# An identity matmul adds the residual, and ScalarE copies the sum out, in the late steps of two attention layers

## The chip, the cores and the metric

The kernel runs on one core of one Trainium2 chip. Five engines work side by side, each through its own instructions in order: TensorE (PE in the profile; its weight loads stand apart as PEld), VectorE (DVE), ScalarE (ACT), GpSimd (POOL) and SyncE (SP), which here only issues transfers (DMA). They meet through semaphores. The metric is device time in microseconds (us): the kernel before takes 1805.18 us, the median of three runs (1801.99 to 1808.54).

## The reference

Four layers on x of 2048 rows by 640 columns: attention, spectral mixing, attention, spectral mixing, each on the layer-normed input and added to it.

```python
def _A_ref(x, wqkv, wo):            # 32 heads of 20; 8 keys per row, 2 rows apart
    q, k, v = (x @ wqkv)...
    logits = einsum("bhsd,bhswd->bhsw", q, kg) * scale
...
    o = einsum("bhsw,bhswd->bhsd", softmax(logits), vg)
    return o @ wo
def _B_ref(x, ...):                 # real part of a 2-D DFT
    a, b = x @ dft_hid_re.T, x @ dft_hid_im.T
    return dft_seq_re @ a - dft_seq_im @ b
x = x + _A_ref(_layernorm(x), A_wqkv, A_wo)
x = x + _B_ref(_layernorm(x), ...)
x = x + _A_ref(_layernorm(x), A_wqkv, A_wo)
x = x + _B_ref(_layernorm(x), ...)
```

## The kernel before

**Data.** The 2048 rows are 4 chunks (c = 0 to 3) of 4 tiles (j = 0 to 3) of 128 rows; a tile is 128 partitions by 640 columns. Products that must be nearly exact are made of reduced-precision operands (fp32r): each operand is split into a high part and a remainder, and three matmuls (PASSES: high x high, high x low, low x high) accumulate in one PSUM bank. A bank holds 512 fp32 columns; they are named by tags (m0, m1, t0, t1, xt, aux0, aux1, pq).

**An attention layer** (`layer_a`, run as layer 0, from about 10 to 400 us, and as layer 2, from about 890 to 1290 us) is a plan of numbered steps. `at(step, phase, fn, ...)` (line 257) puts a piece of work in a step and a phase; a loop then goes through the steps -7 to 66 and, within a step, through the phases in the fixed order below (line 807), and issues every engine's instructions in that order. An engine's queue is therefore the plan read step by step, phase by phase:

```python
"peT0 dma evac hi pe peL pe2 fin red0 dma2 qk sA sB av0 sD red1 sE sC exp evacA actL evacO actl sF av1 qc"
" dmaw dmas misc dmac dmar pe3w pe3"
```

In each step, for a half head group: DVE multiplies q and k windows (L424, reading q from a PSUM copy that ACT makes, `q_copy` L397, phase qc of the step before), POOL halves that product (L426), DVE reduces it to logits (L432); DVE's softmax parts (L447 to L457) stand around ACT's exp (L440, phase exp), DVE multiplies the weights with v (L462), and POOL sums that in three passes (L477 to L479) into the output `oo`. The windows of k and v (`w_load`, L410, five buffers, phase dmaw) and q (`q_load`, L389, which waits for the q copy before it to free the buffer) come by DMA through SP's queue, in order.

**The output product.** A finished chunk of `oo` is transposed on PE (L320, from PSUM back by ACT: L324 the high part, then PE subtracts it by a negative identity, L328, and ACT copies the remainder, L343) into `oT`. `wo_mm` (L502) multiplies a tile of `oT` with the output weights: 15 matmuls of 320 columns for each half, the halves in the two banks aux0 and aux1, then `wo_add` sums the bank and the residual in DVE (`Stats.add`, L152: one instruction for a half, with an accumulator for the row sum) into the residual's tile `xr`, and stores it (L516). The residual comes by `r_load` (L188) or, for chunk 2, with `stage_load` (L488 and L489, into `r1_3`, so that it shows as tile `r`). Then `wo_stats` on ACT (L157 mean, L159 squares, L163), `wo_fin` on POOL (L167 the root), and the normalisation for the next layer: `ln_hi` on ACT (L175, L184 apply, L864 the high part), `ln_lo` on POOL or DVE (L868).

Chunks 0 and 1 go through this early. The **late steps** are those of chunk 2 (tiles 0 to 3 in steps 52 to 55) and of the first two tiles of chunk 3 (steps 60 and 61). Tiles 2 and 3 of chunk 3 follow behind the last step. From step 49 on, PE also runs the next layer's spectral products (`z_mm`, L918, five matmuls of 512 columns at a time, phase pe3, behind everything else of its step); their constants are split by ACT and DVE (L890, L903) in layer 0 and come ready by DMA in layer 2 (L895), into buffers that PE's earlier products must have left. Their order over the steps is written out by hand in `ZTHIRDS`.

In the late steps, a tile with its product in step w has: the product in phase pe3w of w, the sum on DVE in phase misc of w + 1, statistics on ACT in w + 2, the root in w + 3, the normalisation in w + 4 (chunk 2) or w + 3 (chunk 3).

Of the kernel before, what the change touches and what calls it, by code (L numbers as in the profile page):

```python
# [13 lines left out]
AF = mybir.ActivationFunctionType  # L14
# [58 lines left out]
def tile_layers(ctx: ExitStack, tc: tile.TileContext, x, wqkv, wo, cs, wre, wim, out):  # L73
    nc = tc.nc
# [4 lines left out]
    ps = ctx.enter_context(tc.tile_pool(name="ps", bufs=1, space=PSUM))  # L79
# [8 lines left out]
    def T(shape, tag, dt=F32, bufs=1, pool=None):  # L88
        return (pool or sb).tile(shape, dt, tag=tag, name=nm(tag), bufs=bufs)
# [7 lines left out]
    ident = T([P, P], "ident")  # L97
# [32 lines left out]
    class Stats:  # L130
# [18 lines left out]
        def add(self, j, e, xt, ps):  # L149
            o = xt[:, e * 320 : (e + 1) * 320]  # L150
            acc = (self.rstd, self.nmr)[e][:, j : j + 1]
            nc.vector.scalar_tensor_tensor(o, ps, 1.0, o, op0=ALU.mult, op1=ALU.add, accum_out=acc)  # L152

        def added(self, j, xt):
            nmean = self.nmean[:, j : j + 1]
            two = self.sums[:, :, j]
            nc.scalar.activation(two, two, AF.Copy, scale=-1.0 / D, accum_out=nmean)  # L157
            junk = T([P, D], "junk", mybir.dt.bfloat16)
            nc.scalar.activation(junk, xt, AF.Square, bias=nmean, accum_out=self.var[:, j : j + 1])  # L159
            self.var_eps(j)  # L160
# [74 lines left out]
    def layer_a(li, stats, handoff, prev):  # L235
        xin, xout = xs[li], xs[li + 1]
        first = li == 0
        ly = li // 2
        nstats = [None] * NC
# [12 lines left out]
        oT = {}  # L252
        xr = {}
# [3 lines left out]
        def at(step, phase, fn, *args):  # L257
            plan.setdefault((step, phase), []).append((fn, args))
# [32 lines left out]
        def tp(step, kind, c, j, k0, k1, bank, col=0, tag=None):  # L291
            if step not in pieces:
                pieces[step] = []
                at(step, "peT0", pc_pe, step)
                at(step, "hi", pc_hi, step)
                at(step, "peL", pc_sub, step)
                at(step, "actL", pc_lo, step)
            pieces[step].append((kind, c, j, k0, k1, bank, col, tag))
# [194 lines left out]
        def wo_mm(c, j, banks, e0=0, e1=2, k0=0, k1=KD):  # L493
            if e0 == 0 and k0 == 0:
                oT[(c, j, "m")] = []
            for e in range(e0, e1):
# [3 lines left out]
                for i, (a, b) in enumerate(PASSES):  # L500
                    for k in range(k0, k1):
# [5 lines left out]
                            stop=(i, k) == (2, KD - 1),  # L507
                        )

        def wo_add(c, j, e0=0, e1=2):  # L510
            for e in range(e0, e1):
                if e == 0 and j == 0:
                    nstats[c] = Stats()
                nstats[c].add(j, e, xr[(c, j)], oT[(c, j, "m")][e][:, :320])
            if e1 == 2:
                nc.sync.dma_start(xout[c][:, j, :], xr[(c, j)])  # L516
# [172 lines left out]
        while len(gs) < NGRP:  # L689
            if st % 2 == 0 and len(tx) < NC * NJ:  # L690
                c, j = divmod(len(tx), NJ)
# [46 lines left out]
        for c in range(2):  # L738
            for j in range(NJ):
                a = OUTP[ly][c][j]  # L740
                tp(a, "o", c, j, 0, 2, "t1", 0, "s0" if (c, j) == (1, 3) else "ot")
                tp(a, "o", c, j, 2, 5, "t0")
                at(a + 1, "dmar", r_load, c, j, "xa" if (c, j) == (1, 3) else "xr")
                for e in range(2):
                    at(a + 2 + e, "pe2", wo_mm, c, j, ("aux0", "aux1"), e, e + 1)
                    at(a + 3 + e, "misc", wo_add, c, j, e, e + 1)
                at(a + 5, "actl", wo_stats, c, j)
            at(a + 6, "fin", wo_fin, c, 0, 4)
            for j in range(NJ):
                t = LNS[ly][c] + (2 - c) * j  # L750
                if c == 0:
                    at(t, "dma2", handoff.ln_load, c, j)
                else:
                    at(t + STG[0], STG[1], stage_load, c, j)
                at(t, "actl", handoff.ln_hi, c, j, nstats)
                at(t + 1, "misc", handoff.ln_lo, c, j)
        for c, w, xtags in (
            (2, (52, 53, 54, 55), None),
            (3, (60, 61), ("xa", "xa")),
        ):  # L760
            for j in range(NJ):
                if c == 2:
                    tp(48, "o", c, j, 0, 3, ("xt", "t0", "t1", "m0")[j], 0, ("ot", "s1", "r1_2", "r1_2")[j])
                    tp(52, "o", c, j, 3, 5, f"aux{j // 2}", 256 * (j % 2))
                else:
                    tp(58 if j < 2 else TA, "o", c, j, 0, 3, f"aux{j % 2}", 0, ("ot", "s1", "zo0", "zo1")[j])
                    tp(60 if j < 2 else 67, "o", c, j, 3, 5, "aux0" if j < 2 else "pq", 256 * (j % 2))
                if j < len(w):
                    if xtags:
                        at(w[j], "dmar", r_load, c, j, xtags[j])  # L770
                    at(w[j], "pe3w", wo_mm, c, j, ("aux1", "aux0") if c == 3 else ("aux0", "aux1"))
                    at(w[j] + 1, "misc", wo_add, c, j)
                    at(w[j] + 2, "actl", wo_stats, c, j)
                    at(w[j] + 3, "fin", wo_fin, c, j, j + 1)
                    at(w[j] + 3 + (c == 2), "actl", handoff.ln_hi_own, c, j, xr, nstats)
                    at(w[j] + 4 + (c == 2), "misc", handoff.ln_lo, c, j)
# [34 lines left out]
        with tc.manual_schedule(engines=ENGINES):  # L811
            if first:
                prologue_first()
            nc.vector.tensor_copy(mk, mask)
            for s in range(LEAD0[0], last + 1):
                for ph in PHASES:
                    for fn, args in plan.pop((s, ph), ()):
                        fn(*args)
            pc_pe(67)
            pc_hi(67)  # L820
            pc_lo(67, True)
            wo_mm(c, 2, None, 0, 2, 3)
            wo_mm(c, 3, ("pq", "aux0"))
            wo_add(c, 2)
            wo_stats(c, 2)
            wo_fin(c, 2, 3)
            if first:
                handoff.c_hl(14)
            handoff.z_mm(13, None)
            handoff.ln_tail(c, 2, xr, nstats)  # L830
            wo_add(c, 3)
            handoff.ln_lo(c, 2)
            handoff.z_mm(14, None)
            wo_stats(c, 3)
            wo_fin(c, 3, 4)
            if first:
                handoff.c_hl(15)
            handoff.ln_tail(c, 3, xr, nstats)
            handoff.ln_lo(c, 3)
            handoff.z_mm(15, None)  # L840
# [414 lines left out]
    st0 = [None] * NC  # L1255
    b1, b2 = LayerB(1), LayerB(3)
    layer_a(0, st0, b1, None)
    st2 = [None] * NC
    b1.run(st2)
    layer_a(2, st2, b2, b1)  # L1260
    b2.run(None)
    b2.ytile(NT - 1, 0, None)
# [56 lines left out]
```

## Time and profile before

| | us |
|---|---|
| median of three runs | 1805.18 |
| lowest, highest | 1801.99, 1808.54 |
| the profiled execution, its own time | 1805.45 |
| its span, first to last instruction | 1803.7 |
| ACT in the span | 819.3 busy (45%) |
| DMA of the 16 engines, mean | 235 GB/s |

The granted TensorE clock of that execution was 0.992 of full speed on average.

How to read what follows. A row of the page's groups has the line of the kernel, the engine, the operation, output <- input by the kernel's tile names (their numbers left out), the shape and the count, then the busy time of the group and the mean duration of one in ns; matmuls overlap, so busy time divided by count is the distance from one to the next. A row of the timeline has the start in us from the span's start, the duration in us, the engine and the same names; in brackets the idle time just before it and what ended that. A row of the chain of waits has the start, the length and the work that the end was waiting for. A row of the list of waits has the total in us, how many times, and the longest. Fp32 and fp32r operands of PE both show as f32.

### The profile page before, as it was taken

What the parts mean: (1) busy time and instruction counts of PE and PEld (TensorE: products, weight loads), DVE (VectorE), ACT (ScalarE), POOL (GpSimd) and SP (SyncE); (2) the same over time, 40 slices, a digit from 0 to 9 for tenths busy, and PEclk for the clock granted to TensorE, in tenths of its full rate; (3) what the DMA queues carried; (4) which work ended last, traced back from release to release, by engine and by line L of the source; (5) the groups of instructions that cost most, each with busy time, mean ns of one, the idle gap of its engine ahead of it and who ended that gap; (6) DMA issues with size and microseconds to landing.
All of it is one profiled execution on the core that took longest, in us unless ns stands there. A gap on an engine that the chain in (4) does not pass through costs nothing.

```text
span 1803.7 us, 26494 instructions
## 1 busy us (share of the span) xinstructions
PE 1747.6 (97%) x8798; PEld 1508.5 (84%) x8798; DVE 1391.6 (77%) x2135; ACT 819.3 (45%) x1708; POOL 633.2 (35%) x591
## 2 busy tenths in 40 slices
PE   9999997989999999999999999999899999999999
PEld 7879886877888888888888889878787888888888
DVE  5899899988767767768739987899777676676673
ACT  5544644544445445445633334444434443443441
POOL 3799898960000000000018987899300000000000
PEclk9999998999999999999999999999999999999999
DMA  6776667648777887888747866697587766876761
GB/s 233 224 264 208 206 207 249 206 165 284 271 253 247 291 269 247 293 267 266 252 132 231 261 195 194 204 317 251 204 299 251 263 226 219 270 230 223 261 209 52
DMA packets 273994, 423.59 MB, mean 235 GB/s; under 512 B 22688, under 2 KB 153248, under 8 KB 273600
## 3 DMA queue, kind: packets, MB, share of 16 engines
q1 hardware_dynamic: 270656, 419.92, 70.4%
q10 hardware_dynamic: 3200, 1.97, 0.4%
q8 instruction: 70, 1.15, 0.3%
q14 instruction: 68, 0.56, 0.1%
HBM read 336.66 MB, written 85.14 MB: 234 GB/s over the span
## 4 chain that ended last, share of the span: by engine, by line
PE 71%; DVE 12%; DMA 6%; POOL 4%; ACT 3%; issue 3%; SPq 0%; DVEq 0%; ACTq 0%; POOLq 0%
PE m L355 15%; PE aux L996 14%; PE m L1085 10%; PE t L1085 10%; PE pq L1085 5%; PE xt L1085 5%; PE aux L502 4%; DVE pr L424 3%; DVE pr L462 2%; PE m L918 2%; PE t L918 2%; POOL pr L477 1%; DMA qb<-stg 1%; DVE lg L432 1%; DVE s L903 1%
## 5 line engine op out<-in xcount | busy, mean ns | idle before, releaser
L355 PE MATMUL m<-r,s 128*128 128x480 f32 x1920 | 438.7, 383 | 5.2 <-ACT stg L362 2.6
L355 PEld LDWEIGHTS m<-r,s 128*128 128x128 f32 x1920 | 356.4, 189 | 60.8 <-ACT stg L362 4.4
L1078 ACT CAST r<-win 128x512 fp32r<-128x512 f32 x251 | 153.1, 620 | 176.3 <-DVE win L1114 77.6
L167 POOL TENSOR_TENSOR stats<-stats,mhalf 128x1 f32<-128x1 f32 (+1 forms) x40 | 29.1, 728 | 562.6 <-ACT stats L163 562.5
L996 PE MATMUL aux<-r2a,zo 128*128 128x320 f32 x768 | 226.4, 310 | 0.0
L477 POOL TENSOR_TENSOR pr<-pr 128x640 f32<-128x640 f32 x126 | 203.6, 1616 | 42.8 <-DVE pr L462 42.1
L424 DVE TENSOR_TENSOR pr<-pq,win 128x1280 f32<-128x1280 f32 x128 | 189.8, 1483 | 27.4 <-ACT pq L397 26.9
L996 PE MATMUL aux<-pr,zo 128*128 128x320 f32 x704 | 208.2, 309 | 0.0
L1079 DVE TENSOR_TENSOR r<-win,r 128x512 fp32r<-128x512 f32 x251 | 169.6, 688 | 47.2 <-ACT r L1078 46.3
L462 DVE TENSOR_TENSOR pr<-pq,win 128x1280 f32<-128x1280 f32 x128 | 190.9, 1491 | 4.5 <-DVE pq L457 0.2
L426 POOL TENSOR_TENSOR pr<-pr 128x640 f32<-128x640 f32 x128 | 183.3, 1432 | 20.0 <-DVE pr L424 17.0
L1085 PE MATMUL m<-r,r 128*128 128x512 f32 x594 | 153.3, 393 | 0.5 <-ACT r L1078 0.3
L996 PEld LDWEIGHTS aux<-r2a,zo 128*128 128x128 f32 x768 | 144.1, 188 | 2.1 <-issue 0.2
L1085 PE MATMUL t<-r,r 128*128 128x512 f32 x495 | 134.1, 393 | 2.0 <-issue 1.1
L918 PE MATMUL m<-s,r 128*128 128x512 f32 x384 | 121.6, 404 | 15.0 <-DMA s<-c0b 5.7
L996 PEld LDWEIGHTS aux<-pr,zo 128*128 128x128 f32 x704 | 132.2, 188 | 2.0
L1085 PEld LDWEIGHTS m<-r,r 128*128 128x128 f32 x594 | 111.3, 188 | 26.1 <-DVE r L1079 1.0
L918 PE MATMUL t<-s,r 128*128 128x512 f32 x384 | 119.6, 399 | 2.3 <-DVE ot L978 1.5
L478 POOL TENSOR_TENSOR pr<-pr 128x320 f32<-128x320 f32 x126 | 115.0, 913 | 9.9
L362 ACT COPY stg<-m 128x480 f32<-128x480 f32 x128 | 70.9, 556 | 100.2 <-PE m L355 90.0
L1085 PEld LDWEIGHTS t<-r,r 128*128 128x128 f32 x495 | 92.9, 188 | 23.9 <-issue 1.5
L432 DVE TENSOR_REDUCE lg<-pr 128x64 f32<-128x640 f32 x128 | 103.9, 812 | 9.0 <-POOL pr L426 8.8
(270 smaller groups left out, 3244.2 us busy)
## 6 DMA issues: line engine op xcount, KB each, us to landing
win<-cs_in SPq DMA_DIRECT2D x358, 256.0 KB, 4.2
r<-xc SPq DMA_DIRECT2D x240, 256.0 KB, 4.4
win<-kvb SPq DMA_DIRECT2D x96, 440.0 KB, 4.7
xa<-cs_in SPq DMA_DIRECT2D x124, 256.0 KB, 4.2
win<-kvb SPq DMA_DIRECT2D x64, 360.0 KB, 5.2
xc<-stg SPq DMA_DIRECT2D x40, 512.0 KB, 3.1
kvb<-stg SPq DMA_DIRECT2D x60, 320.0 KB, 3.9
xr<-xs SPq DMA_DIRECT2D x40, 320.0 KB, 2.9
```

Source lines behind the costliest of these rows:

```text
L355: nc.tensor.matmul(mt[g][:, : 3 * F], st[:, a, k], wq[q][:, b, k], start=n == 0, stop=n == 14)
L424: nc.vector.tensor_tensor(pr, q, wview(u, jp, 0, [[1, FE]]), op=ALU.mult)
L426: nc.gpsimd.tensor_tensor(pv[:, :, 0:10], pv[:, :, 0:10], pv[:, :, 10:20], op=ALU.add)
L432: nc.vector.tensor_reduce(lgs[u][:, 2 * jp : 2 * jp + 2].rearrange("p j w h -> p (j w h)"), prq.pop((u, jp))[:, :, 0:10], axis=AX.X, op=AL ...
L462: nc.vector.tensor_tensor(pr.rearrange("p j w (h d) -> p j w h d", d=DH), lgs[u][:, 2 * jp : 2 * jp + 2].unsqueeze(4).to_broadcast([P, 2, ...
L477: g.tensor_tensor(pr[:, :, 0:4], pr[:, :, 0:4], pr[:, :, 4:8], op=ALU.add)
L478: g.tensor_tensor(pr[:, :, 0:2], pr[:, :, 0:2], pr[:, :, 2:4], op=ALU.add)
L918: self.last = nc.tensor.matmul(self.z[t][k], self.xn[c][:, a, j, k * P : (k + 1) * P], self.ct[s][:, b], start=s == 0 and i == 0, stop=s = ...
L996: self.last = nc.tensor.matmul(self.ym[e][:, :320], zt[(k, a, ri)][:, j2 * P : (j2 + 1) * P], w[:, e * 320 : (e + 1) * 320], start=(k, a, ...
L1078: nc.scalar.copy(hi, raw)
L1079: nc.vector.tensor_tensor(lo, raw, hi.bitcast(F32), op=ALU.subtract)
L1085: nc.tensor.matmul(bank, w(a, kb), hl[b], start=start and (a, b) == (0, 0), stop=stop and (a, b) == (1, 0),)
```

## The change

For the twelve tiles of the late steps (six in each attention layer) the sum moves. Behind a tile's product PE multiplies the identity with the residual's two halves, in full fp32, into the same banks (`wo_res`, phase pe3w of step w, right behind `wo_mm`). In step w + 1 ACT copies the two halves out with the accumulator for the row sum (`wo_out`, `Stats.copy`), in phase actL in place of DVE's in phase misc, and the tile is stored from there. Chunk 3's residual loads go out two steps earlier and in phase dma. `wo_add` stays for chunks 0 and 1 and for the last two tiles of chunk 3.

```diff
+        def copy(self, j, e, xt, ps):
+            acc = (self.rstd, self.nmr)[e][:, j : j + 1]
+            nc.scalar.activation(xt[:, e * 320 : (e + 1) * 320], ps, AF.Copy, accum_out=acc)
...
+        def wo_res(c, j):
+            for e, m in enumerate(oT[(c, j, "m")]):
+                nc.tensor.matmul(
+                    m[:, :320],
+                    ident,
+                    xr[(c, j)][:, e * 320 : (e + 1) * 320],
+                    start=False,
+                    stop=True,
+                    skip_group_check=True,
+                )
+
+        def wo_out(c, j):
+            if j == 0:
+                nstats[c] = Stats()
+            for e in range(2):
+                nstats[c].copy(j, e, xr[(c, j)], oT[(c, j, "m")][e][:, :320])
+            nc.sync.dma_start(xout[c][:, j, :], xr[(c, j)])
...
                     if xtags:
-                        at(w[j], "dmar", r_load, c, j, xtags[j])
+                        at(w[j] - 2, "dma", r_load, c, j, xtags[j])
                     at(w[j], "pe3w", wo_mm, c, j, ("aux1", "aux0") if c == 3 else ("aux0", "aux1"))
-                    at(w[j] + 1, "misc", wo_add, c, j)
+                    at(w[j], "pe3w", wo_res, c, j)
+                    at(w[j] + 1, "actL", wo_out, c, j)
                     at(w[j] + 2, "actl", wo_stats, c, j)
```

On the engines' queues this takes 24 sums from DVE, puts 24 matmuls on PE and 24 copies on ACT. On ACT the copies of tiles 0 and 2 of chunk 2 stand ahead of a normalisation pair (L184, L864) and of the q copy (L397) of the same step; those of tiles 1 and 3 stand right behind the exp (L440). On SP the store of a tile stands ahead of its step's two window loads, where it stood behind them; POOL's queue is as before.

## The prediction

> **What bounds the kernel now.** I read the engine totals first, then the chain of waits through the two places that the change touches (the late steps of the two attention layers, about 305 to 394 us and 1204 to 1283 us), then each engine's order of time there.
>
> ```profile
> span 1803.7 us, 26494 instructions
> ...
> PE 1747.6 (97%) x8798; PEld 1508.5 (84%) x8798; DVE 1391.6 (77%) x2135; ACT 819.3 (45%) x1708; POOL 633.2 (35%) x591
> ```
>
> ```profile
> 316.00:336.00 20.00, 20.00 (x122) 18.69 (x121) 18.00 (x32) 9.83 (x23) 19.53 (x18) 1.00 0.75 248
> 1204.00:1227.00 23.00, 22.77 (x143) 21.76 (x143) 20.24 (x38) 12.31 (x28) 22.37 (x21) 1.00 0.91 318
> ```
>
> The second fence has two stretches, with PE, PEld, DVE, ACT and POOL busy time in that order. The average says PE. Here PE, POOL and DVE are full together (20.00, 19.53 and 18.00 of 20 us), and ACT has half its time free. So work taken from DVE and given to ACT looks harmless, and work given to PE has no gap to go to while the four tiles of chunk 2 run. What decides is who waits for whom. In the first layer:
>
> ```profile
> 314.04 0.48 DVE L152 SCALAR_TENSOR_TENSOR r<-aux,r 128x320 f32<-128x320 f32 x1
> 314.45 0.08 DVE L152 DVE_READ_ACCUMULATOR r<-aux,r 128x1 f32 x1
> 316.04 0.49 DVE L152 SCALAR_TENSOR_TENSOR r<-aux,r 128x320 f32<-128x320 f32 x1 [1.51 <-PE aux L502]
> ...
> 317.19 1.48 DVE L424 TENSOR_TENSOR pr<-pq,win 128x1280 f32<-128x1280 f32 x1
> ...
> 328.35 0.49 DVE L152 SCALAR_TENSOR_TENSOR r<-aux,r 128x320 f32<-128x320 f32 x1 [1.65 <-PE aux L502]
> ...
> 330.69 1.47 DVE L424 TENSOR_TENSOR pr<-pq,win 128x1280 f32<-128x1280 f32 x1
> ```
>
> DVE already stands still for PE at tiles 0 and 2: PE's output product is late by then, and the chain of waits goes through it:
>
> ```profile
> 309.81 10.60 PE aux L502 x60
> ```
>
> **The price of the new PE work.** Twenty-four matmuls come in (12 tiles, two halves of 320 columns), of full fp32 type; the trace has none. Nearest rows:
>
> ```profile
> L502 PE MATMUL aux<-r2a,r 128*128 128x320 f32 x120 | 18.2, 309 | 0.0
> L502 PEld LDWEIGHTS aux<-r2a,r 128*128 128x128 f32 x120 | 17.9, 188 | 0.4
> L320 PE MATMUL xt<-ident,xa 128*128 128x128 f32 x96 | 14.4, 273 | 1.5 <-ACT xa L184 1.5
> ```
>
> A reduced-precision (fp32r) product of the same shape comes every 18.2/120 = 0.152 us. Lowest: a full fp32 one costs the same, T = 0.30 us for a tile's two. The kernel makes its own near-fp32 products from high and low parts in three such products (PASSES); a complete one has four, 4 x 0.152 = 0.61, T = 1.22. Highest: four products, none with its weight load hidden, 4 x (0.152 + 0.188) = 1.36, T = 2.72. The fp32 transposes, 14.4/96 = 0.150 us for 128 columns, would by their columns give 0.375 for 320, T = 0.75. I take 1.22: what the product has to compute. All 12 tiles together are 12 x 1.22 = 14.6 us of PE.
>
> [...]
>
> **What leaves DVE, and what ACT gets.** A half's sum and accumulator read take 0.41 us from start to next start (314.04 to 314.45), so 0.82 a tile, 4.9 us a layer. For ACT:
>
> ```profile
> 311.78 0.92 ACT L184 ACTIVATE r<-r,stats 128x640 f32<-128x640 f32 x1
> 312.73 0.73 ACT L864 CAST r<-r 128x640 fp32r<-128x640 f32 x1
> 314.16 0.43 ACT L397 COPY pq<-qs 128x320 f32<-128x320 f32 x1 [0.69 <-DVE pr L462]
> ...
> 323.70 0.19 ACT L159 ACTIVATION_READ_ACCUMULATOR junk<-r,stats 128x1 f32 x1
> 323.92 0.20 ACT L163 ACTIVATE stats<-stats 128x1 f32<-128x1 f32 x1
> ...
> 326.86 0.92 ACT L184 ACTIVATE r<-r,stats 128x640 f32<-128x640 f32 x1
> ...
> 329.83 0.42 ACT L397 COPY pq<-qs 128x320 f32<-128x320 f32 x1
> ```
>
> A copy of 128x320 takes 0.42 us, an accumulator read 0.22 (323.70 to 323.92): between 0.42 and 0.64 a half, 0.55 taken, 1.1 a tile. ACT's idle time could hide that. But the copies are queued **ahead** of the normalisation and of the q copy (L397) of the same step, and the q copy is what DVE's next q.k product (L424) reads. Before, a late PE stopped DVE at the end of a step. Now a late PE stops ACT in the middle of it, and behind the waiting copy stand the normalise pair (1.68 us, 311.78 to 313.46), after tile 2 also the statistics (2.97 us from 326.86 to the q copy at 329.83), and the q copy.
>
> **First layer, replayed.** Tile 0: PE's last product ends at 316.04 as before; residual to 317.26; copies done by about 318.0; normalise pair to 319.7; q copy to 320.1. The q.k product starts there and not at 317.19: +2.9 us. Tile 1's copies follow an exp that DVE has delayed by the same 2.9, and PE is done by then: no wait of their own. Tile 2: PE is late by three residuals, 3.66, and about 0.3 for the first bank that ACT frees; its product ended at 328.35, so its residual now ends at about 332.3; copies to 333.2; then the 2.97 us; q copy at 336.2 and not 329.83; the q.k product at 336.6 and not 330.69: +5.9 us. How much of it lasts is POOL's affair, which is full:
>
> ```profile
> 333.41 1.45 POOL L426 TENSOR_TENSOR pr<-pr 128x640 f32<-128x640 f32 x1
> ...
> 342.95 1.94 POOL L477 TENSOR_TENSOR pr<-pr 128x640 f32<-128x640 f32 x1 [0.89 <-DVE pr L462]
> ...
> 357.13 1.55 POOL L477 TENSOR_TENSOR pr<-pr 128x640 f32<-128x640 f32 x1 [0.49 <-DVE pr L462]
> ...
> 381.29 1.93 POOL L477 TENSOR_TENSOR pr<-pr 128x640 f32<-128x640 f32 x1 [1.49 <-DVE pr L462]
> ```
>
> POOL took up that product (ended 332.16) 1.25 us late, at 333.41, so it loses 5.9 - 1.25 = 4.65. Later it waits for DVE only 0.89 + 0.49 + 1.49 = 2.87 us, and DVE is itself late there, but has three more tiles' sums off (2.5 us), most of it while POOL paces; I give back 0.5. First layer: **+4.2 us**. The residuals of chunk 3's two tiles go into PE's later gaps:
>
> ```profile
> 358.14 0.58 PE L328 MATMUL aux<-ot,nident 128*128 128x256 f32 x1 [3.39 <-ACT s L324]
> ...
> 381.18 0.96 PE L918 MATMUL m<-s,r 128*128 128x512 f32 x2 [2.30 <-ACT r L864]
> ```
>
> Two tiles need 2.44, and the gap at 381 is 2.30 with another before it; so they cost nothing. If these gaps went, they would cost 2.4.
>
> **Second layer, replayed the same way**, from PE's, DVE's and ACT's order of time.
>
> ```profile
> 1215.53 4.56 PE L502 MATMUL aux<-r2a,r 128*128 128x320 f32 x30
> ...
> 1250.46 3.73 PE L502 MATMUL aux<-r2a,ot 128*128 128x320 f32 x17 [1.92 <-ACT ot L343]
> ...
> 1268.03 0.73 PE L918 MATMUL m<-s,r 128*128 128x512 f32 x2 [1.96 <-DMA s<-c0b]
> ```
>
> ```profile
> 1221.56 1.48 DVE L424 TENSOR_TENSOR pr<-pq,win 128x1280 f32<-128x1280 f32 x1
> ...
> 1234.51 0.82 DVE L432 TENSOR_REDUCE lg<-pr 128x64 f32<-128x640 f32 x1 [1.83 <-POOL pr L426]
> 1235.25 1.48 DVE L424 TENSOR_TENSOR pr<-pq,win 128x1280 f32<-128x1280 f32 x1
> ```
>
> ```profile
> 1216.99 0.91 ACT L184 ACTIVATE r<-r,stats 128x640 f32<-128x640 f32 x1
> ...
> 1219.96 0.42 ACT L397 COPY pq<-qs 128x320 f32<-128x320 f32 x1
> 1225.22 0.31 ACT L440 ACTIVATE lg<-lg 128x128 f32<-128x128 f32 x1 [4.84 <-DVE lg L451]
> 1225.43 0.28 ACT L175 ACTIVATE stats<-stats 128x1 f32<-128x1 f32 x1
> ...
> 1232.02 0.42 ACT L397 COPY pq<-qs 128x320 f32<-128x320 f32 x1
> ```
>
> Tile 2's product ended at 1215.53 + 4.56 = 1220.1; three residuals later, 1223.7; copies to 1224.5; the 2.97 us to the q copy (1216.99 to 1219.96); q copy at 1227.5; the q.k product at 1227.9 and not 1221.56. The exp behind it comes 3.66 later (1221.56 to 1225.22), at 1231.5; tile 3's copies to 1232.9; the 6.59 us from 1225.43 to 1232.02; q copy at 1239.5; the next q.k product at 1240 and not 1235.25: +4.7 (less than before, because DVE had there waited 1.83 for POOL). From there DVE works without a stop up to the exp that frees ACT for the transposes at 1250.46, so PE starts there 4.7 later, and from there PE is on the chain: two more residuals, 2.44. The wait at 1268.03 is for a load that PE's own progress releases, so it moves along:
>
> ```profile
> SPq L895 <- PE t L918: 7.4, 4, 5.3
> ```
>
> (SP's queue waited 7.4 us in all, 5.3 at most, for PE's spectral products before it could issue such loads.) Second layer: **+7.1 us**.
>
> **What is moved at no cost.** The store of each tile stands on SP's queue ahead of two window loads and no longer behind them; these are needed two steps (some 11 us) later and the copies make them about 5 us late: hidden, but with over 5 us more they would stop DVE. Chunk 3's two residual loads go out two steps earlier; that can only shorten a wait, in a place where PE is the pace. The transposes, POOL's work and the transfers' number stay.
>
> **The sum.** 4.2 + 7.1 = 11.3 on the profiled execution's 1805.45 us (span 1803.7): 1816.8. The median is 1805.18, 0.3 lower, so **1817 us**.
>
> **Rivals.** *Half price* (T = 0.61 to 0.75): three residuals less by 1.8 at tile 2 of each layer and 1.2 less at the end: about 2.4 + 4.1 = 6.5, 1812. For it: the transposes' row. Against: a full product has four partial ones. *Unhidden weight loads* (T = 2.72): 3 x 1.5 = 4.5 more at each layer's tile 2, 3.0 more at the second's end, 1805.45 + 11.3 + 12 = 1829. Against: a weight load of 0.188 us hides behind 0.152 products everywhere else. *PE's gaps take it* (no change): PE idles 3.39 + 2.30 and 1.92 + 1.96 later in the layers, and if ACT's wait passed no further than ACT, 1805 to 1808. Against: the q copy stands behind it. *Faster*: DVE's sums, 4.9 us a layer, and its waits for PE vanish, ACT is never behind; then POOL, which waits for DVE 2.87 us in the first layer taken as the same in the second, takes these gaps back: 1805.45 - 5.7 = 1799.7. It decides once PE's residual is done before ACT comes to the copy, that is with T near 0.3 and PE not late; but DVE's two waits of 1.51 and 1.65 show that PE is late. That the residual stays on DVE is excluded: the order of instructions has no DVE sum left at these tiles.
>
> **How the numbers follow.** Forecast 0.52 (1811 to 1823), half price 0.16, unhidden loads 0.12, gaps take it 0.12, faster 0.08. About 0.3% (5.4 us) is what a measurement of this kernel tells from no change: under 1799.8 is faster, over 1810.6 slower. Faster 0.07; same 0.12 + 0.04 of half price + 0.02 of the forecast + 0.01 = 0.19; slower 0.74. The range takes in the gaps-take-it case and all but the end of the highest price: 1803 to 1828.
>
> **What would show it.** The new matmuls' rows: start to start 1.2 us for a tile, or 0.6, or 2.7. ACT's copies idle "<-PE aux" at tiles 0 and 2 of both layers, then L397 some 3 and 6 us later relative to the products, and DVE's q.k product idle "<-ACT pq". If the copies find PE done, or DVE starts its q.k products no later than POOL wants them, the forecast is wrong in its mechanism; if the waits are there with another length, in T.

## The result, and the profile after

| | us |
|---|---|
| kernel before, median of 4 runs | 1806.71 (1801.99 to 1808.54) |
| changed kernel, median of 4 runs | 1823.49 (1823.10 to 1826.53) |
| ratio | 1.0091, 95% interval 1.0075 to 1.0106 |
| profiled execution after, its own time | 1826.53 |

The change costs 0.9%, some 17 us. The lines of the page that answer to those shown of before:

```profile
span 1824.7 us, 26584 instructions
...
PE 1762.8 (97%) x8846; PEld 1517.5 (83%) x8846; DVE 1379.4 (76%) x2087; ACT 832.2 (46%) x1756; POOL 633.8 (35%) x591
...
L428 DVE TENSOR_TENSOR pr<-pq,win 128x1280 f32<-128x1280 f32 x128 | 189.9, 1484 | 45.9 <-ACT pq L401 43.4
```

(The added functions move the line numbers: the q.k product is L428, the q copy L401, the residual matmul L516, the copy L156, the spectral matmul of the late steps L941; in the experiments up to a few lines off.) DVE has 12 us less work (1391.6 to 1379.4) and the kernel is slower: the last line has DVE idle 45.9 us in front of its q.k products, 43.4 of it for ACT's q copy, where the page of before has

```profile
L424 DVE TENSOR_TENSOR pr<-pq,win 128x1280 f32<-128x1280 f32 x128 | 189.8, 1483 | 27.4 <-ACT pq L397 26.9
```

Where that is new shows in the list of DVE's waits from 294 to 405 us, before and then after (total, how often, longest):

```profile
DVE r L152 <- PE aux L502: 3.2, 2, 1.7
DVE s L903 <- ACT s L890: 2.7, 2, 2.1
...
DVE pr L424 <- ACT pq L397: 0.9, 1, 0.9
```

```profile
DVE pr L428 <- ACT pq L401: 8.4, 3, 3.2
DVE s L926 <- ACT s L913: 6.8, 3, 3.1
```

The wait for PE (3.2 us) is gone from DVE; in its place stands one for the q copy (0.9 to 8.4), and one for the spectral constants that ACT casts grew from 2.7 to 6.8. The timeline of ACT around tiles 0 and 2 of the first layer says why:

```profile
316.44 0.44 ACT L156 ACTIVATE r<-aux 128x320 f32<-128x320 f32 x1 [4.57 <-PE aux L516]
...
317.40 0.91 ACT L188 ACTIVATE r<-r,stats 128x640 f32<-128x640 f32 x1
...
318.98 0.42 ACT L401 COPY pq<-qs 128x320 f32<-128x320 f32 x1
...
330.41 0.62 ACT L913 CAST s<-stg 128x512 fp32r<-128x512 f32 x1 [3.21 <-DMA stg<-cs_in]
331.22 0.44 ACT L156 ACTIVATE r<-aux 128x320 f32<-128x320 f32 x1 [0.20 <-PE aux L516]
...
335.15 0.42 ACT L401 COPY pq<-qs 128x320 f32<-128x320 f32 x1
```

And DVE's first two q.k products behind them:

```profile
319.43 1.49 DVE L428 TENSOR_TENSOR pr<-pq,win 128x1280 f32<-128x1280 f32 x1 [3.24 <-ACT pq L401]
...
335.60 1.49 DVE L428 TENSOR_TENSOR pr<-pq,win 128x1280 f32<-128x1280 f32 x1 [3.12 <-ACT pq L401]
```

At tile 0 ACT stands 4.57 us for PE's residual, then does two copies, the normalise pair and only then the q copy. At tile 2 it stands 3.21 us for the load of spectral constants that it casts ahead of the copies, and after that only 0.20 us for PE: there the two limits end almost together. (SP issued that load at 325.62 us, in the kernel before at 322.04.) The products start at 319.43 and 335.60, before at 317.19 and 330.69: +2.24 and +4.91 us.

To see where the whole distance arises, the same matmul is looked up in both profiled executions: the first spectral one behind the first layer's output products, a transpose before the second layer's late steps, and the first spectral one at that layer's end. Before, then after:

```profile
400.77 0.62 PE L918 MATMUL m<-s,r 128*128 128x512 f32 x2
...
1180.00 0.49 PE L320 MATMUL xt<-ident,zo 128*128 128x128 f32 x3
...
1288.95 0.62 PE L918 MATMUL m<-s,r 128*128 128x512 f32 x2
```

```profile
405.04 0.62 PE L941 MATMUL m<-s,r 128*128 128x512 f32 x2
...
1195.97 0.49 PE L324 MATMUL xt<-ident,zo 128*128 128x128 f32 x3
...
1308.51 0.62 PE L941 MATMUL m<-s,r 128*128 128x512 f32 x2
```

The distances are 4.27, 15.97 and 19.56 us, and 21.1 at the end (spans 1824.7 and 1803.7, before rounding). So the first layer's late steps make 4.3, the second's 3.6, and 11.7 us come between them, where nothing was changed. How much of that belongs to the change is looked at below with other executions.

### The profile page after: what moved, and what is told of

Its sections match the earlier page's. It is cut to its first block, busy times and chain, and to the rows that moved or that the text cites. A ratio compares the mean times of both kernels' runs of the same rounds, so it can differ in the third digit from the quotient of the medians.

```text
span 1824.7 us, 26584 instructions
## 1 busy us (share of the span) xinstructions
PE 1762.8 (97%) x8846; PEld 1517.5 (83%) x8846; DVE 1379.4 (76%) x2087; ACT 832.2 (46%) x1756; POOL 633.8 (35%) x591
## 4 chain that ended last, share of the span: by engine, by line
PE 65%; DVE 13%; DMA 12%; ACT 4%; issue 3%; POOL 3%; SPq 0%; DVEq 0%; ACTq 0%; POOLq 0%
PE m L359 17%; PE aux L1019 11%; PE t L1108 9%; PE m L1108 9%; PE aux L506 5%; PE pq L1108 5%; PE xt L1108 4%; DMA xc<-stg 3%; DMA win<-cs_in 3%; DVE pr L428 2%; DVE pr L466 1%; PE m L941 1%; DVE r L1102 1%; DMA s<-c0b 1%; POOL pr L481 1%
## 5 line engine op out<-in xcount | busy, mean ns | idle before, releaser
L428 DVE TENSOR_TENSOR pr<-pq,win 128x1280 f32<-128x1280 f32 x128 | 189.9, 1484 | 45.9 <-ACT pq L401 43.4
L941 PE MATMUL m<-s,r 128*128 128x512 f32 x384 | 123.6, 409 | 16.4 <-DMA s<-c0b 6.5
L941 PE MATMUL t<-s,r 128*128 128x512 f32 x384 | 118.8, 397 | 2.3 <-DVE ot L1001 1.5
```

The lines of the kernel that those rows point to most:

```text
L428: nc.vector.tensor_tensor(pr, q, wview(u, jp, 0, [[1, FE]]), op=ALU.mult)
L941: self.last = nc.tensor.matmul(self.z[t][k], self.xn[c][:, a, j, k * P : (k + 1) * P], self.ct[s][:, b], start=s == 0 and i == 0, stop=s = ...
```

## The experiments

Twelve kernels ran, in three groups; the runs of one group share a chip and the runs of the kernel before.

| kernel | median | before beside it | ratio, 95% interval |
|---|---|---|---|
| first group: residual loads early, nothing else | 1808.95 | 1811.43 | 0.9985 (0.9973 to 0.9997) |
| no residual matmuls | 1822.08 | 1811.43 | 1.0051 (1.0032 to 1.0071) |
| copies behind the q copy | 1822.60 | 1811.43 | 1.0062 (1.0041 to 1.0083) |
| residual on PE, sum on DVE | 1817.13 | 1811.43 | 1.0026 (1.0012 to 1.0039) |
| second group: store behind the window loads | 1820.90 | 1811.03 | 1.0058 (1.0040 to 1.0076) |
| the same, no residual matmuls | 1814.60 | 1811.03 | 1.0015 (1.0003 to 1.0027) |
| first layer only | 1819.36 | 1811.03 | 1.0047 (1.0030 to 1.0064) |
| second layer only | 1813.21 | 1811.03 | 1.0012 (1.0002 to 1.0023) |
| third group: changed kernel again | 1828.73 | 1811.80 | 1.0100 (1.0084 to 1.0115) |
| store behind the window loads, again | 1826.72 | 1811.80 | 1.0088 (1.0074 to 1.0102) |
| tiles 1 and 3 only | 1815.94 | 1811.80 | 1.0030 (1.0017 to 1.0044) |
| residual matmuls twice | 1833.24 | 1811.80 | 1.0127 (1.0110 to 1.0144) |

One warning stands ahead of the reading. "Store behind the window loads" ran twice, the same kernel on the same chip, and gave 1820.90 and 1826.72 in two groups, while the kernel before moved by 0.8. The intervals above hold within a group. Between groups a difference of 6 us says nothing, and a distance to the neighbour before can be off by some 5: this kernel's was 9.9 us in one group and 14.9 in the other.

**The early residual loads alone.** Of the change only the moved loads of chunk 3's residual are kept; the sums stay on DVE.

```diff
-                        at(w[j], "dmar", r_load, c, j, xtags[j])
+                        at(w[j] - 2, "dma", r_load, c, j, xtags[j])
```

> Only the earlier residual loads of chunk 3 are kept; sums stay on DVE as in the kernel before. Every theory: the same time as before, within 3 us; the DVE wait of 1.1 us for that load in the second layer goes, where PE is the pace. If it is slower by 5 us or more, the loads are part of the loss.

Measured 1808.95, 2.5 us under the kernel before, and the only kernel that was not slower than its neighbour before; the interval leaves out 1 by 0.0003 only. None of the loss comes from this part.

**No residual matmuls.**

```diff
-                    at(w[j], "pe3w", wo_res, c, j)
                     at(w[j] + 1, "actL", wo_out, c, j)
```

> The changed kernel without the residual matmuls; ACT's copies stay where they are, so the residual is left out of the twelve tiles. Queue theory (what is lost is that ACT's copies wait for a late PE ahead of the q copy): PE is less late (by 1.08 us a tile) but ACT still waits for the product at tiles 0 and 2, so 2 to 5 us above before. PE theory (the time is PE's added work, 12 x 1.08 = 13 us, and ACT's order does not matter): no more than before, 1802 to 1808. Elsewhere theory (most of the loss is made in stages that the change does not touch, by where short idle times fall): anything from 1800 to 1825, and the lag in the late steps small.

Measured 1822.08: +10.7 us over before, +13.1 over the run with early loads. The queue theory's +2 to +5 and the PE theory's range both miss. The total fits only the widest forecast, that of losses made elsewhere, and that one wanted a small lag in the late steps, where the first layer alone makes 6.1 us (table below). So with no new PE work at all a loss is still there; how large it is stays uncertain, because the other run without these matmuls (below, with the store moved as well) is only 3.6 us over its neighbour before. DVE's q.k products at the same two places:

```profile
318.72 1.49 DVE L428 TENSOR_TENSOR pr<-pq,win 128x1280 f32<-128x1280 f32 x1 [2.54 <-ACT pq L401]
...
333.66 1.49 DVE L428 TENSOR_TENSOR pr<-pq,win 128x1280 f32<-128x1280 f32 x1 [2.00 <-ACT pq L401]
```

They are 1.53 and 2.97 us behind the kernel before, against 2.24 and 4.91 in the changed kernel. PE's output product is late without the residual already (the prediction's 1.51 and 1.65 us of DVE waiting show it), and at tile 0 it now stops ACT, 2.21 and 1.67 us at the two copies, with the q copy behind. At tile 2 of this run ACT does not wait for PE; it waits 2.38 us for the constants' load, as before (2.21), so the 2.97 are tile 0's delay and, for the larger part of the rest, the copies' own time of 0.83.

**The sum back on DVE, the residual matmuls kept.**

```diff
                     at(w[j], "pe3w", wo_res, c, j)
-                    at(w[j] + 1, "actL", wo_out, c, j)
+                    at(w[j] + 1, "misc", wo_add, c, j)
```

> The residual matmuls stay on PE, the sums return to DVE's old place at the end of step w + 1, so the twelve tiles hold the residual twice. Queue theory: PE's lateness now stops DVE only at the end of a step, as before the change: tile 0 costs 1.1 us and tile 2 3.2 us of DVE in each layer, with the last two tiles' 2.2 us on PE in the second: 5 to 9 us above before, 1811 to 1815. PE theory: 13 us or more above before, 1819 or more, as the changed kernel.

Measured 1817.13: +8.2 us over the run with early loads, so the 24 matmuls cost 8 us when it is DVE that waits for them, of 13 us of PE time. Over the kernel before it is +5.7, inside the queue theory's +5 to +9 and far from the PE theory's 13 or more; in absolute time, which took a faster kernel before, it lies between the two forecasts. The two halves, 13.1 for the copies without residual and 8.2 for the residual without copies, less 2.5 for the loads, make 18.8, against 16.8 and 16.9 measured for the whole in other groups.

**Copies behind the q copy.**

```diff
-                    at(w[j] + 1, "actL", wo_out, c, j)
+                    at(w[j] + 1, "misc", wo_out, c, j)
```

> The changed kernel with ACT's copies in phase misc of step w + 1, behind the normalisation and the q copy, where DVE's sums stood. Queue theory: the q copies come at their old distance, DVE's q.k products wait for ACT less than 1 us, and at least half of the loss in the late steps (4.3 us in the first layer) goes: 1808 to 1815. PE theory: as the changed kernel, 1820 to 1826. Elsewhere theory: the late steps improve, the total does not follow.

With the copies the tile's store moves too, behind its step's window loads. Measured 1822.60: nothing won that can be told. By its number the queue theory's forecast (1808 to 1815) is wrong and the PE theory's (1820 to 1826) right, so the total alone does not show that the order of the queue matters. The list of DVE's waits from 294 to 405 us says where the gain went in the first layer:

```profile
DVE s L926 <- ACT s L913: 14.2, 4, 6.0
DVE pr L428 <- ACT pq L401: 3.9, 2, 2.0
```

The wait for the q copy fell from 8.4 to 3.9 (under 1 us was expected), but DVE now waits 14.2 us for the spectral constants that ACT casts (6.8 in the changed kernel and in its repetition). ACT in turn waits for their load:

```profile
ACT s L913 <- DMA stg<-cs_in: 25.1, 7, 6.2
```

That is 13.6 us in the changed kernel and 22.2 in its repetition. At tile 2 the loads go out on SP's queue right behind the store, which waits for ACT's late copies (the stores' waits for ACT r L156 are 23.4 us in all, 17.5 in the changed kernel):

```profile
334.42 0.32 SPq L530 DMA_DIRECT2D xs<-r  x1
334.80 0.92 SPq L908 DMA_DIRECT2D stg<-cs_in  x2
```

Before, the two stood at 328.87 and 329.24 us. SP also waits for DVE to free the staging buffer (L908 <- DVE s L926, 1.6 us, and 1.6 in the changed kernel); the two causes were not separated. In the second layer ACT casts no such constants, and there the order shows: DVE's waits for the q copy are 1.2 us instead of 8.8, and the layer adds -0.2 us where the changed kernel's adds 3.6 (table below).

**The store behind the window loads.** The copies stay where the change put them; the store goes back to phase misc, behind the step's window loads. The expectation has it behind the loads of the constants as well, but those are in phase dmac, which follows misc, so in this kernel too they stand behind the store, as they did in the kernel before.

```diff
                 nstats[c].copy(j, e, xr[(c, j)], oT[(c, j, "m")][e][:, :320])
+
+        def wo_store(c, j):
             nc.sync.dma_start(xout[c][:, j, :], xr[(c, j)])
...
                     at(w[j] + 1, "actL", wo_out, c, j)
+                    at(w[j] + 1, "misc", wo_store, c, j)
```

> The changed kernel with one thing put back: the store of a tile goes to SP's queue behind its step's window loads and loads of spectral constants, where it stood before the change (in the changed kernel it stands ahead of them and waits there for ACT's copies). The residual matmuls and ACT's copies stay. Store theory (the store holds SP's queue, so the constants' loads go out late, and ACT's cast of them, which stands ahead of the copies and of the q copy, waits): most of the loss goes, +4 to +9 us over the kernel before on the same chip, ACT's waits for stg<-cs_in back to 2 us or less at tile 2, while its waits for PE aux stay. Queue theory (late PE and the copies themselves ahead of the q copy): no change, +13 to +19. PE theory: no change, +13 to +19.

Measured 1820.90, +9.9 us and so between the store theory's forecast and that of the other two; 1.0058 against the 1.0091 measured first looked like 6 us for the store. So it was repeated beside the changed kernel:

> The changed kernel with the store of a tile behind its step's loads on SP's queue, once more, now beside the changed kernel on the same chip. Store theory (the place of the store costs about 6 us): 4 to 8 us below the changed kernel. If the earlier difference was one of chips: within 3 us of it.

> The changed kernel once more, on the chip of the runs that follow. Every theory: 1.0075 to 1.0106 of the kernel before, as measured first; +13 to +19 us. It is the base for the other three.

Measured 1826.72 beside 1828.73: 2.0 us, with overlapping intervals. Ahead of or behind the window loads, the store's place is worth little, if anything, and the first comparison was one between groups. What the store theory names, that a store waiting for the copies holds up the constants' loads behind it, no run took away; it stays open.

**The store behind the window loads, no residual matmuls.**

> As the run before (store back in its old place, ACT's copies kept), and without the 24 residual matmuls: the residual of the late steps is left out of the sum. Store theory: as fast as the kernel before or a little faster, -5 to +3 us. Queue theory with the copies' own time as the cost (0.8 us ahead of the q copy at two tiles of a layer): +5 to +10 us, as the earlier run without the residual. PE theory: -5 to +3 as well, so this run tells the first two apart and the run before tells the first from the third.

Measured 1814.60, +3.6 us over before (interval 0.5 to 4.9) and 6.3 us under its neighbour with the residual in the same group. The +3.6 is just over the -5 to +3 of the store and PE theories and under the queue theory's +5 to +10. Its trace still has DVE waiting 7.4 us for the q copy in the first layer's late steps. The 6.3 is the second measure of what the 24 matmuls cost (8.2 and 6.3). That this run is 7.5 under the earlier one without them can't be read as the store's price, for the reason just given.

**Tiles 1 and 3 only.**

```diff
-                    at(w[j], "pe3w", wo_res, c, j)
-                    at(w[j] + 1, "actL", wo_out, c, j)
+                    if j % 2:
+                        at(w[j], "pe3w", wo_res, c, j)
+                    at(w[j] + 1, *(("actL", wo_out) if j % 2 else ("misc", wo_add)), c, j)
```

> The change on tiles 1 and 3 only (of chunk 2, and tile 1 of chunk 3); tiles 0 and 2 are summed on DVE as before. Copies that stand ahead of the q copy (tiles 0 and 2) are gone, half of the residual matmuls and half of the early stores stay. Queue theory: nearly all of the loss is at tiles 0 and 2, so -3 to +4 us over the kernel before, and DVE's waits for the q copy (8.4 us in the first layer's late steps of the changed kernel) back under 3 us. PE and store theories: half of the loss, +6 to +10.

Measured 1815.94: +4.1 us over before by medians, at the edge of the queue theory's +4, and +5.4 by the ratio (3.1 to 8.0), which reaches into the +6 to +10 of the other two. It is 12.8 us under the changed kernel beside it (1828.73). So about three quarters of the loss come with the tiles whose copies stand ahead of the q copy, though they are half the tiles, half the matmuls and half the stores. DVE's wait in the first layer's late steps:

```profile
DVE pr L428 <- ACT pq L401: 2.0, 2, 1.6
```

2.0 us and not 8.4, as the queue theory had it (under 3).

**The residual matmuls twice.**

```diff
                     at(w[j], "pe3w", wo_res, c, j)
+                    at(w[j], "pe3w", wo_res, c, j)
```

> The changed kernel with every residual matmul issued twice (the residual is counted twice in the sum of the late steps): 24 more matmuls, 13 us more of PE time by 0.54 each. PE theory (PE paces these steps, each us of PE is a us of time): +11 to +14 us over the changed kernel. Queue theory (it counts where ACT and DVE wait for PE: three tiles' residuals, 3.2 us, ahead of each layer's tile 2, and the second layer's end): +5 to +9. If the gaps take it: 0 to +3.

Measured 1833.24, +4.5 us for 13 us more of PE work: under all of the PE theory's range and just under the queue theory's. Its two q.k products:

```profile
321.60 1.49 DVE L428 TENSOR_TENSOR pr<-pq,win 128x1280 f32<-128x1280 f32 x1 [5.48 <-ACT pq L401]
...
339.93 1.49 DVE L428 TENSOR_TENSOR pr<-pq,win 128x1280 f32<-128x1280 f32 x1 [4.49 <-ACT pq L401]
```

2.17 and 4.33 us later than in the changed kernel, where the PE time added ahead of the copies is 1.07 at tile 0 and 3.2 at tile 2 (the residual of tile 0 also began 1.08 later, see the rows further down): here all of it is passed on. Of the 13 us added in all, the rest of the run takes some two thirds back.

**One layer at a time.**

```diff
-                    at(w[j], "pe3w", wo_res, c, j)
-                    at(w[j] + 1, "actL", wo_out, c, j)
+                    if first:
+                        at(w[j], "pe3w", wo_res, c, j)
+                    at(w[j] + 1, *(("actL", wo_out) if first else ("misc", wo_add)), c, j)
```

> The change in the first attention layer alone; the second is as before. If what the change costs is made in place and carried on: +3 to +7 us over the kernel before, and the distance to it stays the same from 400 us on. If a delay made in the first layer grows in the unchanged spectral stage and the next layer's early steps (from 400 to 1180 us): +11 to +17, with the growth there. Elsewhere theory (that growth is where short idle times fall, whatever is changed): growth of 4 to 12 us there in this run and in the next one too.

> The change in the second attention layer alone; the first is as before. Made in place: 0 us of distance to the kernel before up to about 1195 us, then +3 to +8. If the growth between 400 and 1180 us follows from the first layer's delay, there is none here and the total is +3 to +8. Elsewhere theory: distance of 4 to 12 us already at 1180, total +8 to +18, although nothing up to there differs from the kernel before.

Measured +8.3 and +2.2 us, together 10.5 where both at once cost 16.8 and 16.9 in other groups. The first lies between the two forecasts of a loss made in place (+3 to +7) and of one that grows (+11 to +17), the second just under all of its forecasts. The traces of these two, and of the others, against the profiled execution before, by the same matmuls as in the section on the result (us made in each stretch, matched matmul by matmul, one execution of each):

| execution | first layer's late steps, 290 to 401 | unchanged, 401 to 1180 | second layer, 1180 to 1289 | behind |
|---|---|---|---|---|
| early loads only | -0.1 | 5.0 | -1.8 | -0.2 |
| second layer only | -0.4 | 6.3 | 1.7 | -1.2 |
| first layer only | 7.3 | 8.4 | -2.9 | -0.2 |
| changed kernel | 4.3 | 11.7 | 3.6 | 1.5 |
| changed kernel again | 7.9 | 9.2 | 3.2 | 2.5 |
| residual matmuls twice | 10.8 | 9.1 | 7.0 | 1.3 |
| tiles 1 and 3 only | 2.5 | 10.0 | -1.6 | -0.4 |
| store behind the window loads | 6.5 | 11.7 | 2.5 | 1.1 |
| the same, again | 5.4 | 8.7 | 4.4 | 1.4 |
| the same, no residual matmuls | 4.0 | 5.0 | -3.4 | 1.1 |
| no residual matmuls | 6.1 | 8.9 | 2.2 | 1.0 |
| residual on PE, sum on DVE | 3.4 | 9.9 | -1.3 | -1.2 |
| copies behind the q copy | 9.4 | 10.4 | -0.2 | 1.8 |

Two executions of one kernel differ by up to 3.6 us in a stretch (rows 4 and 5), so only large differences count. The first two rows have the first layer as before and yet 5.0 and 6.3 us in the unchanged stretch: the profiled execution of before was a good one there. Most of that arises at one place, near 910 us, by 3.1 and 4.0; the last section shows it, a longer idle time of PE (1.85 and 1.84 us, before 0.91) and behind it 13 matmuls that take 4.65 and 5.29 us and not 3.10. The changed kernel's distance grows there too, by 2.8 us (0.9 in its repetition), and that part can't be put down to the change.

What follows the change stands right behind the first layer: from 445 to 503 us the changed kernel's distance grows by 3.7 us, by 3.8 to 4.4 in the rows of the first layer only, the changed kernel again and the doubled matmuls, and by 0.0 and 1.5 in the first two. In PE's timeline of the changed kernel:

```profile
463.61 0.74 PE L941 MATMUL m<-s,r 128*128 128x512 f32 x2 [0.41 <-DVE s L926]
...
495.12 0.94 PE L1108 MATMUL m<-r,r 128*128 128x512 f32 x3 [1.23 <-DVE zo L1001]
...
497.18 0.94 PE L1108 MATMUL t<-r 128*128 128x512 f32 x3 [0.42 <-DVE ot L1001]
```

Before, PE has none of these waits: 2.06 us in these three lines, for DVE, which there prepares the next stage's operands. Why DVE is late was not tried. The other 5 us of the 11.7 are in part the TensorE clock: in the unchanged stretch the execution before has no time at half clock, the changed kernel has 3.41 us of it three times, from 924 us (last section) and here (PE's busy time, the granted clock, the transfers):

```profile
599.70:603.00 3.30, 3.30 (x9) 0.50 1.03 361
1009.30:1012.60 3.30, 3.15 (x8) 0.50 0.96 370
```

3.41 us at a clock of 0.50 and not 1.00 are 1.7 lost where PE is the pace, an estimate from these rows (in the stretch from 924 us 13 matmuls took 1.56 longer), so by it these two make up to 3.4 of the 5. Whether a delayed layer makes such stretches more likely can't be told from one execution of each kernel.

## Why the prediction was right, point by point

The forecast was 1817 us and slower; it is 1823.49. The mechanism, ACT's copies queued ahead of the q copy and stopped by a late PE, is what the trace shows at three of the four places: ACT waits for PE 4.57 us at tile 0 of the first layer, 3.17 and 2.50 at tiles 0 and 2 of the second. At tile 2 of the first layer it waits 0.20 for PE and 3.21 for the constants' load, a wait that the prediction has not. That the total came within 7 us is in part luck: of the profiled 21.1 us the two layers made 7.9, where 11.3 were forecast, and the rest arose where the prediction has nothing. The sizes:

- **T, the price of a tile's residual.** Taken 1.22 us, measured 1.07: the doubled run's row is 2.31 us for 8 records where the changed kernel's is 1.24 for 4.

```profile
315.70 1.24 PE L516 MATMUL aux<-r,ident 128*128 128x320 f32 x4
```

```profile
316.78 2.31 PE L516 MATMUL aux<-r,ident 128*128 128x320 f32 x8
```

  Half price (0.61 to 0.75) and unhidden weight loads (2.72) are both excluded by this. That a full fp32 matmul costs four products of the reduced type, 4 x 0.152 = 0.61 us, was the author's estimate, and half of it for the half price; no run shows of how many products it is made. 0.535 is measured.
- **The copies.** Taken 1.1 us a tile, measured 0.96 at tile 0 (316.44 to 317.40).
- **First layer.** Predicted +2.9 and +5.9 at the two q.k products, +4.2 kept; measured +2.24, +4.91 and +4.3. The same code in two further executions kept 7.3 and 7.9, so the agreement to 0.1 is luck; the replay holds to some 4 us. At tile 2 it has the residual end at 332.3, by the trace it ends at 331.73, so the late PE was sized well, and the constants' load took as long. That chunk 3's residuals fall into PE's later gaps is borne out: PE's distance does not grow there (4.52 us at the transposes of 344.03 in the execution before, 4.27 at the products of 394.36).
- **Second layer.** The replay's own steps hold. DVE's q.k products at tile 2 and behind tile 3, of the changed kernel:

```profile
1244.80 1.49 DVE L428 TENSOR_TENSOR pr<-pq,win 128x1280 f32<-128x1280 f32 x1 [3.70 <-ACT pq L401]
...
1256.55 1.49 DVE L428 TENSOR_TENSOR pr<-pq,win 128x1280 f32<-128x1280 f32 x1
```

  Against 1221.56 and 1235.25 before they are 23.24 and 21.30 later. The last product ahead of tile 0's copies shows how late the layer came in (before, then after):

```profile
1202.11 1.48 DVE L424 TENSOR_TENSOR pr<-pq,win 128x1280 f32<-128x1280 f32 x1
```

```profile
1218.33 1.48 DVE L428 TENSOR_TENSOR pr<-pq,win 128x1280 f32<-128x1280 f32 x1
```

  That is 16.22, so the layer added 7.0 and 5.1, predicted 6.3 and 4.7. What failed is the step after: the wait at 1268.03 "moves along", and two more residuals add 2.44. PE's timeline at the two places that had waits of 1.92 and 1.96 us:

```profile
1270.72 4.55 PE L506 MATMUL aux<-r2a,ot 128*128 128x320 f32 x30
...
1289.18 0.73 PE L941 MATMUL m<-s,r 128*128 128x512 f32 x2 [0.39 <-DMA s<-c0b]
```

  Both waits went (0 and 0.39), 3.5 us taken back, so 3.6 were left and not 7.1. Against the two executions whose second layer is as before (-1.8 and -2.9) it is about 6. The layer costs next to nothing in the run with the sum on DVE (-1.3) and in that with the copies behind the q copy (-0.2), so a later PE alone, or the copies at the end of the step, cost it little. The two runs without residual matmuls make 2.2 and -3.4 there, which leaves open what the copies alone cost it.
- **The sum.** It carried a delay unchanged through all that lies behind. That is the term that was missing, and the main reason why 1817 was too low: some 3 us grew right behind the first layer, 1.5 behind the second, and the clock took more in this execution than in that before (10.2 us at half clock in the unchanged stretch, there none).
- **What makes the loss.** The prediction put it on the residuals' time: eight of them make 9.8 of its 11.3 us. The runs without them keep +10.7 and +3.6 us: the output product was late before, and the move of the sum to ACT alone lets it stop the q copy. The residual's own share is 6.3 to 8.2 us.
- **The store.** Called hidden with a limit of 5 us more. In the first layer no DVE wait for a window of over 0.2 us is there; in the second one of 2.16 appears, <- DMA win<-kvb, at 1283.08. The changed kernel and the one with the store put back differ by 2.0 us, too little to tell. That the constants' loads stand behind the store was not weighed.
- **Rivals.** "Gaps take it" falls: the q copy does pass the wait on. "Faster" falls by its own condition, PE not late: even without residual matmuls it is late.

The place is shown: tiles 0 and 2, by the run that leaves them out. The order, ACT's copies ahead of the q copy, is borne out in the second layer, by one execution of the run that puts them behind it (DVE's wait 1.2 and not 8.8 us); in the first layer that run gained nothing, and the order is argued there from the waits. How the loss splits is known only roughly: 6.3 to 8.2 us for the residual matmuls, 3.6 to 10.7 for the copies without them. Open are some 2 to 5 us in the unchanged stretch, the store's 0 to 6 us and the constants' loads behind it, and why one layer at a time adds up to 6 us less than both, which the spread between groups could make.

## What to carry to other kernels

Work moved to a half-idle engine can cost what stands behind it in that engine's queue (ACT was busy for 45% of the span, and DVE's q.k products behind its copies came 2.24 and 4.91 us later): look for what a late input would hold up there, not for the engine's idle time. An engine that was late for a cheap waiter can become expensive when the waiter is changed, even if it gets no new work (+10.7 and +3.6 us without the residual matmuls). And a difference of 0.3% between kernels that ran at different times says nothing until both ran side by side (one kernel gave 1820.90 and 1826.72 us).

## What the runs showed of the hardware

A full fp32 matmul stands in the trace as two records (48 of L516 for 24 matmuls), each 0.27 us behind the last (2.31 less 1.24 us for four records more), so 0.535 us for 320 columns; the fp32r one of this shape comes every 0.152 us (18.2 us for 120 in the kernel before).

In one comparison a gap of PE that was 1.20 us longer was followed by matmuls that took 1.56 us longer. At this place of an unchanged stage PE's idle before a group of matmuls is 0.91 us in the profiled execution before and 2.11 in that after, both for ACT:

```profile
909.32 0.71 PE L355 MATMUL m<-r,s 128*128 128x480 f32 x2 [0.91 <-ACT s L225]
...
910.92 3.10 PE L355 MATMUL m<-r,s 128*128 128x480 f32 x13 [0.57 <-ACT s L225]
```

```profile
922.02 0.71 PE L359 MATMUL m<-r,s 128*128 128x480 f32 x2 [2.11 <-ACT s L229]
...
923.62 4.66 PE L359 MATMUL m<-r,s 128*128 128x480 f32 x13 [0.57 <-ACT s L229]
```

The same 13 matmuls take 3.10 and 4.66 us. In the view of stretches what follows in the execution after is:

```profile
922.00:923.00 1.00, 0.98 (x5) 1.00 0.00 0
923.00:924.00 1.00, 0.43 (x3) 0.96 0.00 0
924.00:925.00 1.00, 1.00 (x4) 0.50 0.00 0
```

The clock falls to half. In the execution before, behind its shorter gap:

```profile
912.00:913.00 1.00, 1.00 (x7) 1.00 0.06 16
```

It stays at 1.00. In the execution after it went to half behind gaps of 2.11 and 0.57 us with some 1 us of work between. But the length of the gaps alone does not decide. At the same place, the run with the store moved and no residual matmuls, then that with the matmuls twice:

```profile
917.29 0.71 PE L359 MATMUL m<-r,s 128*128 128x480 f32 x2 [1.83 <-ACT s L229]
...
918.89 3.10 PE L359 MATMUL m<-r,s 128*128 128x480 f32 x13 [0.57 <-ACT s L229]
```

```profile
927.55 0.71 PE L359 MATMUL m<-r,s 128*128 128x480 f32 x2 [1.83 <-ACT s L229]
...
929.15 4.65 PE L359 MATMUL m<-r,s 128*128 128x480 f32 x13 [0.57 <-ACT s L229]
```

The same two gaps, 1.83 and 0.57 us, are followed once by 3.10 us for the 13 matmuls, as at the full clock of the execution before, and once by 4.65, as with the half clock of the execution after. With early loads only and with the second layer only the 13 take 4.65 and 5.29 us, about half of the 3.1 and 4.0 us that those two lose near there; most of the rest is the longer gap (1.85 and 1.84 us). The changed kernel's three stretches at half clock between 401 and 1180 us each last 3.41 us and begin at 599.65, 923.92 and 1009.25 us; what sets their starts was not shown.
